# Angle tables through two matmuls, a gate with its key sums side by side, and constants built once, in an attention and long-convolution kernel

## The chip, the cores and the metric

One core of a Trainium2 chip runs the whole program. The core has five engines that work side by side, each through its own queue in order: PE (TensorE, matmuls), ACT (ScalarE, activations and copies), DVE (VectorE), POOL (GpSimd) and SP (SyncE), which here issues all transfers. The metric is the device time of one execution in microseconds (us).

## The reference

Inputs are q, k, v of shape (4, 8, 768, 64), w_proj (512, 1536), filter_fft (768, 512) and w_out (512, 512), all float32. The first half is block attention: each query may look at its own block of 64 keys and at the three earlier blocks whose mean key fits it best. The second half is a gated long convolution over the sequence.

```python
k_rep = k.reshape(B, H, n_blocks, 64, D).mean(axis=3)
gate = np.einsum('bhsd,bhnd->bhsn', q, k_rep)        # causal blocks only, others -1e9
top_idx = np.argsort(gate, axis=-1)[..., -3:]        # plus the query's own block
scores = where(mask & causal, scale * q @ k.T, -1e9)
x = softmax(scores) @ v                              # heads merged: (4, 768, 512)
x1, x2, x3 = split(x @ w_proj)
x2_conv = irfft(rfft(x2, axis=1) * rfft(filter_fft, axis=0))
out = (x1 * x2_conv * x3) @ w_out
```

## The kernel before

**Attention.** The work is cut into 16 groups: one batch and one pair of heads each, 768 queries and keys, 128 partitions. For each group the kernel transposes keys on PE (L368), sums each block of 64 keys on DVE (`ks`, L371), copies keys to a slot (`kt`, L381, on ACT), and does the like for queries (L432; high fp16 part `qh` L435 on ACT, low part `ql` L438 on DVE). Scores are matmuls (L568), the exponential is on ACT (L575), the causal triangle is cut by POOL (L580), and the values are multiplied on PE (L598) and normalised on DVE (L611).

**The gate.** Key sums are kept as a high and a low fp16 part in `km`; queries likewise in `qx`. For each group `e_gate` runs 20 matmuls (L490): five chunks of 128 queries, and for each the four products high-high, high-low, low-high and low-low, summed in one PSUM bank over 24 columns (12 blocks of two heads). `e_max` (L503 to L509) writes a large negative number over the blocks that aren't causal, in PSUM, and takes the eight largest of each row; `e_lt` (L516, L521) compares with the third largest and writes a mask of zeros and ones. The mask is transposed (L538) into 12 spare rows of the query slot (`qt`, L545). The key slot has the block pattern `eblk` in the same 12 rows, filled once with -30720 on the block's own columns (L206 to L209, copied by L226), so the score matmul adds the mask. Four slots of each kind exist. The first nine groups (`tm=9`) go this way; the last seven let DMA do the transposes (L470, L474).

**The tables.** `F` holds sines and cosines for a DFT of length 768, folded to 384 rows. Six pieces of 128 x 384 are made at the start, each in five steps: a matmul of row and column numbers gives the angle in units of 1/768 turn (e1, L253); multiply by 1/768 and add 2^23, which rounds to whole turns (e2, L258 on ACT or L261 on DVE); subtract 2^23 (e3, L267); angle minus 768 times the turns (e4, L272, DVE); sine (e5, L276, ACT). The steps e2 to e4 keep float32 in `prod` buffers. An exponential may start only when all of `F` is there, since sine and exponential need different tables on ACT.

**The convolution.** Each group's result goes through sums and differences (L636) and table matmuls (L648, L655) to a spectrum `XT`. When four groups, one batch, are there, the batch is projected (L757), multiplied with the filter's spectrum (L766, DVE), combined (`Y`, L776, POOL), transformed back (L820), combined again (`ce` L829, `sd` L835) and multiplied with the gating products (L793, L799, L802) into `yT` (L841, POOL or DVE), then projected out (L851), copied (L855) and stored (L858).

**The order.** A list scheduler in the kernel's Python, `plan`, orders all operations before the program is built. Each operation has a priority time `vt`, counted in groups, with a weight for its kind (`v_...`), a cost per engine, and for some kinds a choice of engine with a penalty for DVE (`d_...`). `ahead` bounds how far beyond the current score step operations may be taken. Buffers are pools with fixed counts (`POOLS`); PSUM has eight banks of which four serve all but the scores while attention runs. Until `warm_until` of planned time, `filler` puts matmuls of zeros (L952) where PE would have nothing to do.

Of the kernel before, what the change touches and what calls it, by code (L numbers as in the profile page):

```python
# [16 lines left out]
P = 128  # L17
# [15 lines left out]
MAGIC = float(2 ** 23)  # L33
# [11 lines left out]
for _pi, _segs in enumerate(PIECES):  # L45
# [6 lines left out]
    direct=2, tm=9, kin=16, p0=-2.58, p1=0.359, pvlag=-1.081, dlag=1.538, dlen=1.485, h0=4.836,  # L52
    hlen=3.401, f0=-0.546, f1=4.97, ld=-1.042, s2a=-0.355, s2b=0.464, x0=0.446, x1=1.137, c0=0.817,
    c1=1.054, o0=1.347, ahead=16.341, delta=0.011, queue=6.283, w0=1.608, wl=1.643, wlag=-7.304, warm_until=34.129,
    tr0=-26.33, trl=16.468, fill0=1.323, v_yT=1.15, v_sd=-2.381, d_k2=3.845, v_trig=4.775, v_ldq=-0.068, v_max=-6.527,
    v_g=2.311, v_Y=0.82, v_k2=0.404, v_rec=-2.613, v_small=3.535, v_gate=-0.028, v_km=1.623, d_x1=-0.346, d_shQ=0.734,
    v_xT=-2.135, v_prod=-3.254, v_ldv=-0.43, d_yT=0.279, v_ks=0.928, v_osb=-3.052, v_ldk=-0.329, v_kT=0.038, v_gT=3.039,
    d_md=0.144, d_trig=0.482, v_qT=0.017, v_mT=-0.085, v_lt=-3.096, v_fe=1.769, d_eo=0.005, v_md=0.045, v_phase=-0.03,
    v_shQ=2.489, v_ldf=0.595, d_Y=5.668, v_sel=-5.514, v_warm0=3.241, v_x1=-0.983, v_ldw=-0.146, v_tab=6.693, v_va=1.68,
    v_iota=-1.707, d_XT=-0.476, v_qh=0.233, v_h0=0.611, v_eblk=4.461, v_id32=1.695, v_st=2.959, v_nyq=-2.837, v_s2=0.062,  # L60
    v_st1=0.023, v_XT=0.064, v_t=-9.103, v_ql=1.449, v_hf=0.158, d_g=6.58, d_ce=8.444, d_osb=2.444, d_fill=0.427,
    v_w=-0.555, v_ce=-1.909, v_fill=-0.339, v_op=1.026, v_pv=-1.989, d_w=4.395, v_nrm=-0.253, v_ha=-5.02, v_id16=-0.109,
    v_eo=1.933, v_x13=-0.231, d_fe=-4.145, v_cv=-1.548, v_sc=0.113, v_T2=-0.349, v_T1=2.226, d_qh=2.343, v_pq=-4.162,
    d_pq=6.99, v_ex=0.251, a0=0.0, o1=1.0, pen_dve=0.205, late=2.0,
)

POOLS = dict(kn=2, qn=3, vn=2, k2=1, qx=4, ks=2, km=3, m8=2, nm=1,
# [16 lines left out]
class Op:  # L84
    __slots__ = ("i", "eng", "emit", "deps", "bufs", "alloc", "vt", "lock", "size", "tag",
                 "start", "done", "on", "pre", "nd", "succ", "ready")


class Graph:
# [3 lines left out]
    def add(self, tag, vt, eng, emit, rd=(), wr=(), res=(), lock=False, size=0):  # L93
        o = Op()
        vt += self.par.get("v_" + tag, 0.0)
        o.i, o.tag, o.vt, o.eng, o.emit, o.lock, o.size = len(self.ops), tag, vt, eng, emit, lock, size
        deps = set()
# [43 lines left out]
def build(par):  # L141
# [21 lines left out]

    def cviews(x):
        cv = x.rearrange("p (g n) -> p g n", g=2)
        return (cv[:, :, 0:256].rearrange("p g (k n) -> p g k n", k=2),
                cv[:, :, 256:HS].rearrange("p g (k n) -> p g k n", k=2))

    def e_warm0(E, nc, en):
        nc.vector.memset(E.warm, 0.0)  # L170
        nc.vector.memset(E.colv, 0.0)
        nc.vector.memset(E.rowv, 0.0)

    def e_phase(E, nc, en):
        ph = E.colv[32:33, :]
        nc.vector.memset(E.rowv[32:33, :], 1.0)
        nc.vector.memset(ph, 192.0)
        for x_ in cviews(ph):
            nc.vector.memset(x_[:, :, 1, :], 0.0)
        nc.vector.memset(ph[:, P:P + 1], 192.0)  # L180
        nc.vector.memset(E.magic, MAGIC)
        nc.vector.memset(E.nmagic, -MAGIC)
# [14 lines left out]
    add("warm0", T0 - 1, {"DVE": (0.6, 0.75)}, e_warm0, wr=[cb("warm"), cb("cols"), cb("phase")])  # L197
    add("tab", T0 - 1, {"ACT": (1.5, 1.6)}, e_tab, rd=[cb("warm")], wr=[cb("tab")])
    add("phase", T0, {"DVE": (1.62, 1.7)}, e_phase, wr=[cb("phase"), cb("magic")])
# [4 lines left out]
    def e_eblk(E, nc, en, h=0):  # L204
        x = E.eblk[64 * h:64 * h + 64, :]
# [6 lines left out]
    for h in range(2):  # L212
        add("eblk", T0 + 3 + h, {"POOL": pol(2.48)}, lambda E, nc, en, h=h: e_eblk(E, nc, en, h), wr=[(cb("eblk"), h)])

    slot_init = []
    for i in range(POOLS["kt"]):
# [5 lines left out]
        def e_fk(E, nc, en, i=i):  # L222
            eng = nc.vector if en == "DVE" else nc.gpsimd
            for h in range(2):
                r = slice(0, 64) if h == 0 else slice(64, 76)
                eng.tensor_copy(E.t["kt"][i][r, :, h, :], E.eblk[r, :].rearrange("p (c s) -> p c s", s=P))  # L226
# [4 lines left out]
                rd=[(cb("eblk"), 0), (cb("eblk"), 1)], wr=[(cb(("slot", i)), 1)], lock=True)])  # L231
# [13 lines left out]
    for t in range(HC):  # L245
        for hf in range(2):
            vt = par["tr0"] + par["trl"] * (0.33 * t + 0.16 * hf)
            pr, kk = psb(), Buf("prod")
            ka, kb = (kk, 0), (kk, 1)
# [5 lines left out]

            def e2(E, nc, en, pr=pr, kk=kk):
                if en == "ACT":
                    nc.scalar.activation(E.sb(kk)[:, 0:HS], E.bk(pr)[:, 0:HS], AF.Identity,  # L258
                                         bias=E.magic, scale=1.0 / S)
                else:  # L260
                    nc.vector.tensor_scalar(E.sb(kk)[:, 0:HS], in0=E.bk(pr)[:, 0:HS], scalar1=1.0 / S,  # L261
                                            scalar2=MAGIC, op0=ALU.mult, op1=ALU.add)

            def e3(E, nc, en, kk=kk):
                o, i_ = E.sb(kk)[:, HS:S], E.sb(kk)[:, 0:HS]
                if en == "ACT":
                    nc.scalar.activation(o, i_, AF.Identity, bias=E.nmagic, scale=1.0)  # L267
                else:
# [899 lines left out]
```

## Time and profile before

| | |
|---|---|
| median of 6 runs | 235.57 us (235.25 to 235.79) |
| profiled execution | 235.63 us, span 233.9 us |
| busy: PE, DVE, ACT, POOL | 227.3, 193.7, 174.6, 170.9 us |
| clock granted to PE | full in all of the span |
| DMA | 40.9 MB, 76.7% of 16 engines' span |
| PE fillers (L952) | 143, the last at 34.9 us |
| first exponential | 22.75 us |
| last matmul ends | 230.1 us |

The span runs from the first instruction to the last of one execution; the execution's own time is 1.7 us longer. Busy time counts an instruction from its start to its end, so overlapping ones make PE look fuller than its rate: 20 gate matmuls have a mean of 173 ns each, and together take 0.49 us.

### The profile page before, as it was taken

What the parts mean: (1) busy time and instruction counts of PE and PEld (TensorE: products, weight loads), DVE (VectorE), ACT (ScalarE), POOL (GpSimd) and SP (SyncE); (2) the same over time, 40 slices, a digit from 0 to 9 for tenths busy, and PEclk for the clock granted to TensorE, in tenths of its full rate; (3) what the DMA queues carried; (4) which work ended last, traced back from release to release, by engine and by line L of the source; (5) the groups of instructions that cost most, each with busy time, mean ns of one, the idle gap of its engine ahead of it and who ended that gap; (6) DMA issues with size and microseconds to landing.
All of it is one profiled execution on the core that took longest, in us unless ns stands there. A gap on an engine that the chain in (4) does not pass through costs nothing.

```text
span 233.9 us, 6574 instructions
## 1 busy us (share of the span) xinstructions
PE 227.3 (97%) x2370; PEld 157.7 (67%) x2370; DVE 193.7 (83%) x617; ACT 174.6 (75%) x288; POOL 170.9 (73%) x312
## 2 busy tenths in 40 slices
PE   8998999999999999999999999999999999999993
PEld 6897877777765777777656767776566677545551
DVE  6788988888799999899898889888996887596850
ACT  3989999999989889897967886967575656414243
POOL 8848967776549999998599999674699652169720
PEclk9999999999999999999999999999999999999999
DMA  6999996999999999999999999516185210512016
GB/s 179 320 233 226 236 243 189 228 195 211 247 221 223 266 211 235 243 188 176 264 217 275 166 261 169 123 36 158 49 169 160 67 34 3 168 53 86 0 45 224
DMA packets 120224, 40.92 MB, mean 175 GB/s; under 512 B 114304, under 2 KB 114304, under 8 KB 120192
## 3 DMA queue, kind: packets, MB, share of 16 engines
q1 hardware_dynamic: 120192, 40.51, 76.7%
q8 instruction: 18, 0.29, 0.5%
q14 instruction: 14, 0.11, 0.2%
HBM read 24.64 MB, written 6.29 MB: 132 GB/s over the span
## 4 chain that ended last, share of the span: by engine, by line
PE 78%; ACT 12%; DVE 4%; issue 2%; DMA 2%; POOL 0%; ACTq 0%; DVEq 0%; POOLq 0%; SPq 0%
PE ps L793 17%; PE ps L568 12%; PE ps L851 9%; PE ps L757 8%; PE ps L598 7%; PE ps L820 7%; ACT ex L575 6%; PE ps L952 5%; PE ps L648 4%; PE ps L368 3%; ACT kt L381 3%; PE ps L490 2%; PE ps L655 2%; DMA kn<-in_k_dram 2%; ACT qx L435 1%
## 5 line engine op out<-in xcount | busy, mean ns | idle before, releaser
L575 ACT ACTIVATE ex<-ps 128x1024 f16<-128x1024 f32 (+1 forms) x96 | 85.0, 924 | 10.4 <-PE ps L568 9.6
L580 POOL TENSOR_SCALAR_AFFINE_SELECT ex<-ex 128x256 f16<-128x256 f16 x96 | 42.9, 452 | 22.4 <-ACT ex L575 20.5
L568 PE MATMUL ps<-qt,kt 76*128 76x512 f16 (+7 forms) x256 | 49.8, 305 | 0.3
L776 POOL TENSOR_TENSOR Y<-t,t 128x512 f16<-128x512 f32 (+1 forms) x32 | 40.5, 1271 | 11.9 <-DVE t L766 10.9
L793 PE MATMUL ps<-xT,wp 128*128 128x384 f16 x256 | 48.9, 326 | 0.0
L381 ACT CAST kt<-ps 64x384 f16<-64x384 f32 x64 | 30.3, 474 | 9.9 <-PE ps L368 8.0
L793 PEld LDWEIGHTS <-wp 128*128 128x128 f16 x256 | 24.1, 98 | 14.2 <-issue 0.2
L568 PEld LDWEIGHTS <-kt 76*128 76x128 f16 (+1 forms) x256 | 23.4, 97 | 14.8 <-issue 1.0
L598 PEld LDWEIGHTS <-ex 128*128 128x128 f16 x672 | 25.2, 97 | 4.0 <-issue 0.9
L598 PE MATMUL ps<-va,ex 128*128 128x65 f16 x672 | 26.6, 193 | 0.3 <-DVE qt L545 0.2
L855 ACT COPY osb<-ps 128x512 f32<-128x512 f32 x24 | 14.1, 589 | 16.9 <-PE ps L851 16.8
L841 POOL TENSOR_TENSOR yT<-prod,sd 128x384 f16<-128x384 f32 x23 | 23.3, 1026 | 4.0 <-DVE prod L802 2.6
L851 PE MATMUL ps<-wo,yT 128*128 128x512 f16 x96 | 23.3, 379 | 0.0
L757 PE MATMUL ps<-wp,XT 128*128 128x512 f16 x96 | 23.2, 379 | 0.1
L802 DVE TENSOR_TENSOR prod<-ps,x 128x384 f32<-128x384 f32 x32 | 17.7, 553 | 5.1 <-PE ps L793 3.4
L952 PE MATMUL ps<-warm 128*128 128x256 f16 x143 | 20.5, 290 | 1.1 <-DVE warm L170 1.1
L371 DVE TENSOR_REDUCE ks<-ps 128x6 f32<-128x384 f32 x32 | 17.3, 550 | 2.2 <-ACT kt L381 1.7
L611 DVE TENSOR_TENSOR xn<-ps,rec 128x384 f16<-128x384 f32 x32 | 17.8, 556 | 0.9
L820 PE MATMUL ps<-G,Y 128*128 128x384 f16 x96 | 18.2, 326 | 0.0
L835 DVE TENSOR_TENSOR sd<-ce,ps 128x384 f32<-128x384 f32 x32 | 16.1, 550 | 2.0 <-ACT ce L829 1.3
L952 PEld LDWEIGHTS <-warm 128*128 128x128 f16 x143 | 14.6, 104 | 4.0 <-DVE warm L170 1.1
L766 DVE TENSOR_TENSOR t<-ps,HA 128x512 f32<-128x512 f32 x24 | 16.4, 685 | 0.9 <-PE ps L757 0.4
(109 smaller groups left out, 397.9 us busy)
## 6 DMA issues: line engine op xcount, KB each, us to landing
kn<-in_k_dram SPq DMA_DIRECT2D x32, 192.0 KB, 3.8
qn<-in_q_dram SPq DMA_DIRECT2D x32, 192.0 KB, 3.7
vn<-in_v_dram SPq DMA_DIRECT2D x16, 384.0 KB, 4.7
out_dram<-osb SPq DMA_DIRECT2D x24, 256.0 KB, 2.1
t<-in_moe_w_proj_dram SPq DMA_DIRECT2D x12, 256.0 KB, 3.9
t<-in_moe_filter_fft_dram SPq DMA_DIRECT2D x6, 256.0 KB, 4.6
qt<-qx SPq DMA_DIRECT2D x14, 96.0 KB, 3.6
t<-in_moe_w_out_dram SPq DMA_DIRECT2D x4, 256.0 KB, 4.1
```

Of the source, the lines that this page charges most:

```text
L381: (nc.scalar.copy if en == "ACT" else nc.vector.tensor_copy)(E.sb(Kt[g])[r, HC * hf:HC * (hf + 1), 1 - t, :], E.bk(kp)[r, 0:HS].rearrange( ...
L568: nc.tensor.matmul(o[:, col:col + w], lhsT=E.sb(Kt[g])[0:KR[t], kc, 1 - t, :], rhs=E.sb(Qt[g])[0:KR[t], q0 // P:(q0 + w) // P, 1 - t, :], ...
L575: nc.scalar.activation(E.sb(ex)[:, 0:w], E.sp(sp)[:, 0:w], AF.Exp, scale=ESC)
L580: nc.gpsimd.affine_select(out=dv, in_=dv, compare_op=ALU.is_ge, fill=0.0, base=0, pattern=[[0, 2], [1, P]], channel_multiplier=-1)
L598: nc.tensor.matmul(o[:, 65 * c:65 * c + 65], lhsT=E.sb(exs[pi])[:, col:col + P], rhs=E.sb(va[g])[:, t, kc, :], start=(kc == 0), stop=(kc = ...
L757: nc.tensor.matmul(E.bk(xa), lhsT=w, rhs=E.wp[:, j, Dm:2 * Dm], start=(j == 0), stop=(j == NP - 1))
L776: (nc.vector if en == "DVE" else nc.gpsimd).tensor_tensor(E.sb(Y)[ro, n_, :], E.sb(x)[ri, :], E.sb(y)[ri, :], op=op)
L793: nc.tensor.matmul(E.bk(xq)[:, 0:HS], lhsT=E.wp[:, d2, 2 * Dm * m + P * dc:2 * Dm * m + P * (dc + 1)], rhs=E.sb(xT[gs[d2]])[:, cs], start= ...
L820: nc.tensor.matmul(E.bk(cv)[:, 0:HS], lhsT=E.sb(Y)[:, 3 * p_ + n_, P * dc:P * (dc + 1)], rhs=E.G[:, 3 * p_ + n_, :], start=(n_ == 0), stop ...
L841: (nc.vector if en == "DVE" else nc.gpsimd).tensor_mul(E.sb(yT)[:, dc, cs], E.sb(prod)[:, cs], E.sb(sd)[:, cs])
L851: nc.tensor.matmul(E.bk(op_), lhsT=E.sb(yT)[:, d2, P * c:P * (c + 1)], rhs=E.wo[:, d2, :], start=(d2 == 0), stop=(d2 == NP - 1))
L952: nc.tensor.matmul(E.ps[:, 3584:3840], lhsT=E.warm[:, 0:P], rhs=E.warm[:, 0:256], start=True, stop=True)
```

## The change

*Tables.* A row of ones times 1536 turns is added to the angle by the first matmul (row 64 of `rowv` holds 1536 and rows 64 to 127 of `colv` hold 768). Divided by 768 and written as fp16, the value lies between 1024 and 2048, where fp16 has whole numbers only, so the write rounds to whole turns. A second matmul with -768 times the identity (`nid`) subtracts them in PSUM, and the sine reads PSUM. The rounded turns take an `x1` buffer in place of `prod`.

*Gate.* High and low key sums are the 48 columns of one operand, so a chunk takes two matmuls. A DVE reduction adds the two halves into a new SBUF tile `gs` (two buffers), on which the masking, MAX8 and comparison then work.

*Constants.* `eblk` has 64 rows instead of 128, is built once, and its rows are copied to the second half of the slots too. The fillers' operand is cleared ahead of all else.

*The plan.* Nearly every weight in `PAR` is another (a few are in the diff below). The cost model adds 0.115 us where ACT or DVE goes on to another partition quadrant, and some costs are changed.

```diff
-    hlen=3.401, f0=-0.546, f1=4.97, ... ahead=16.341, ... warm_until=34.129,
-    ... d_trig=0.482, ... d_yT=0.279, ... d_x1=-0.346, ... d_osb=2.444
+    hlen=3.36, f0=-1.155, f1=7.084, ... ahead=46.953, ... warm_until=32.306,
+    ... d_trig=6.615, ... d_yT=8.721, ... d_x1=3.233, ... d_osb=6.098
...
+    add("nid", T0 + 2.05, {"DVE": dve(64)}, lambda E, nc, en: nc.vector.tensor_scalar_mul(E.nid, E.id32, -float(S)),
+        rd=[cb("id32")], wr=[cb("nid")], lock=True)
...
-        nc.vector.memset(E.warm, 0.0)
-        nc.vector.memset(E.colv, 0.0)
+        nc.vector.memset(E.colv[0:64, :], 0.0)
+        nc.vector.memset(E.colv[64:P, :], float(S))
...
+        nc.vector.memset(E.rowv[64:65, :], TURNS)
...
-    for h in range(2):
-        add("eblk", T0 + 3 + h, {"POOL": pol(2.48)}, lambda E, nc, en, h=h: e_eblk(E, nc, en, h), wr=[(cb("eblk"), h)])
+    add("eblk", T0 + 3, {"POOL": pol(2.48)}, e_eblk, wr=[cb("eblk")])
...
-                r = slice(0, 64) if h == 0 else slice(64, 76)
-                eng.tensor_copy(E.t["kt"][i][r, :, h, :], E.eblk[r, :].rearrange("p (c s) -> p c s", s=P))
+                n_ = 64 if h == 0 else NB
+                eng.tensor_copy(E.t["kt"][i][64 * h:64 * h + n_, :, h, :],
+                                E.eblk[0:n_, :].rearrange("p (c s) -> p c s", s=P))
...
             def e2(E, nc, en, pr=pr, kk=kk):
                 if en == "ACT":
-                    nc.scalar.activation(E.sb(kk)[:, 0:HS], E.bk(pr)[:, 0:HS], AF.Identity,
-                                         bias=E.magic, scale=1.0 / S)
+                    nc.scalar.activation(E.sb(kk), E.bk(pr)[:, 0:HS], AF.Copy, bias=0.0, scale=1.0 / S)
...
+            def e3(E, nc, en, pr=pr, kk=kk):
+                nc.tensor.matmul(E.bk(pr)[:, 0:HS], lhsT=E.nid, rhs=E.sb(kk), start=False, stop=True,
+                                 skip_group_check=True)
+            def e5(E, nc, en, t=t, cs=cs, pr=pr):
+                nc.scalar.activation(E.F[:, t, cs], E.bk(pr)[:, 0:HS], AF.Sin, bias=0.0, scale=TWO_PI / S)
...
-                for n_, (lo, w) in enumerate(((0, 0), (0, 1), (1, 0), (1, 1))):
+                for lo in range(2):
                     col = P * (2 * (c - 1) + lo) if by_dma else S * lo + P * c
-                    nc.tensor.matmul(o[:, 32 * c:32 * c + 24], lhsT=E.sb(qs)[:, col:col + P],
-                                     rhs=E.sb(km)[:, w, 0:24], start=(n_ == 0), stop=(n_ == 3))
+                    nc.tensor.matmul(o[:, 64 * c:64 * c + 48], lhsT=E.sb(qs)[:, col:col + P],
+                                     rhs=E.sb(km)[:, 0:2, :], start=(lo == 0), stop=(lo == 1))
...
+            nc.vector.reduce_sum(x, o[:, :, 0:48].rearrange("p c (w n) -> p c n w", w=2), axis=AX.X)
+            nc.vector.memset(bass.AP(tensor=h, offset=off + 3, ap=[[row, 64], [26, 5], [12, 2]]), NEG)
...
-                    nc.vector.max(E.sb(m8)[:, c - 1, t, :], gv[:, c - 1, 12 * t:12 * t + n])
+                    nc.vector.max(E.sb(m8)[:, c - 1, t, :], x[:, c - 1, 12 * t:12 * t + n])
...
+        if e in quad and quad[e] != o.quad:
+            occ, vis = occ + 0.115, vis + 0.115
...
     with tc.manual_schedule():
+        nc.vector.memset(E.warm, 0.0)
         for o in order:
             o.emit(E, nc, o.on)
```

## The prediction

> **What bounds the kernel now.** I read four views, from coarse to fine. First the page's busy lines, then its 40 slices (one digit is 5.8 us, 9 means 90% or more):
>
> ```profile
> PE 227.3 (97%) x2370; PEld 157.7 (67%) x2370; DVE 193.7 (83%) x617; ACT 174.6 (75%) x288; POOL 170.9 (73%) x312
> PE   8998999999999999999999999999999999999993
> ACT  3989999999989889897967886967575656414243
> ```
>
> PE looks like the bound everywhere. But its 97% holds filler matmuls that compute nothing, and ACT is just as full in the first third. The groups by line give the filler and the rows that the change touches (columns: busy us, mean ns, idle time before):
>
> ```profile
> L952 PE MATMUL ps<-warm 128*128 128x256 f16 x143 | 20.5, 290 | 1.1 <-DVE warm L170 1.1
> L490 PE MATMUL ps<-km,qx 128*128 128x24 f16 x320 | 10.5, 173 | 0.0
> L509 DVE MAX8 m<-ps 128x8 f32<-128x8 f32 (+2 forms) x160 | 13.5, 161 | 0.6
> L267 ACT ACTIVATE prod<-prod,nmagic 128x384 f32<-128x384 f32 x6 | 3.3, 617 | 0.0
> L272 DVE SCALAR_TENSOR_TENSOR prod<-prod,ps 128x384 f32<-128x384 f32 x6 | 3.1, 553 | 0.6 <-ACT prod L267 0.6
> L276 ACT ACTIVATE F<-prod 128x384 f16<-128x384 f32 x6 | 2.9, 524 | 0.0
> ```
>
> All 143 fillers lie before 35 us; at 0.109 us each (the chain has 40 of them in 4.37 us) they fill 15.6 us of that time. The busy times by stretch (PE, PEld, DVE, ACT, POOL; then clock, DMA share, GB/s) show where each engine is the limit:
>
> ```profile
> 5.00:38.00 33.00, 32.22 (x356) 26.89 (x355) 27.79 (x96) 31.34 (x59) 25.02 (x49) 1.00 1.03 256
> 38.00:75.00 37.00, 36.16 (x487) 26.74 (x485) 32.40 (x126) 36.00 (x60) 25.22 (x55) 1.00 1.05 215
> 75.00:225.00 150.00, 149.95 (x1492) 99.01 (x1491) 128.82 (x374) 102.24 (x163) 116.48 (x199) 1.00 0.67 148
> ```
>
> Up to 38 us PE's work is largely filler and ACT is busy 31.3 of 33 us: ACT, with DVE behind it, sets the pace. From 38 to 75 us PE and ACT are both full. From 75 us to the last matmul at 230.1 us PE alone is. The chain of work that ended last says so for the end, all on PE:
>
> ```profile
> 222.34 2.60 PE ps L793 x16
> 224.94 5.19 PE ps L851 x24
> 230.14 0.03 ACTq L855
> ```
>
> So two things shorten this kernel: an earlier moment at which PE is full (38 us), and less PE work after it.
>
> **What the Trainium skill says.** (1) "TensorE: Matmul & The Clock Gate", section "Wait — 56ns, not 53.3ns?": matmuls start N/2.4 GHz + 2.5 ns apart, but never closer than about 25 ns. The trace agrees: the chain has "L490 x20" at 0.49 us, 24.5 ns each with 24 columns. With 48 columns the formula gives 22.5 ns, still under the floor, so a matmul twice as wide costs the same. (2) "ScalarE: Activation LUTs", section "What ACT_TABLE_LOAD costs": a per-partition bias operand adds about 93 ns. The trace: L258 (bias operand, float32 out) starts every 0.47 us, L435 (same size, no bias operand, 16-bit out) every 0.38 us. (3) "VectorE: DVE Perf Modes", table "The perf-mode tier table": tensor_reduce runs at one element per cycle at best. L371 agrees: 384 elements, 0.50 us from start to start, so about 0.10 us beside the 0.40 us of elements.
>
> **The change, part by part.**
>
> *Gate matmuls (L490).* Twenty per group become ten of 48 columns: 16 groups x 10 x 24.5 ns = 3.9 us of PE. By stretch there are 60, 80 and 180 matmuls before 38, in 38-75 and after 75 us, that is 3, 4 and 9 groups. The first three run among fillers: worth nothing. The nine save 9 x 0.245 = 2.2 us on the path. The four save 1.0 us of PE where ACT has only 1.0 of 37 us free; I count half, 0.5 us. Sum: 2.7 us.
>
> *Angle tables.* Before, each of six pieces was one matmul (L253), then multiply-and-round (L258 on ACT x4, L261 on DVE x2), subtract the constant (L267, ACT), multiply-add (L272, DVE), sine (L276, ACT). After: matmul, one fp16 copy, matmul with -768 times the identity, sine out of PSUM. ACT before, from start to start: 4 x 0.465 + 6 x 0.507 + 6 x 0.41 = 7.4 us. After, if all six copies go to ACT (the planner's penalty for DVE on these, d_trig, rises from 0.48 to 6.6): 12 x 0.38 = 4.6 us, from row L435. That is 2.8 us less on ACT; with two copies left on DVE, 3.6. DVE loses 6 x 0.50 + 2 x 0.50 = 4.0 us. PE gains 6 x 0.163 = 1.0 us between 6 and 15 us, where it runs 47 fillers between 9 and 15 us: nothing, as long as fillers are there. ACT was busy 16.6 of 17.4 us from its first key copy (5.39 us) to the first exponential (22.75 us), so most of the 2.8 us comes through. The change adds a wait: PE must wait for the copy before the second matmul, and behind it on PE stand the transposes of the first groups, which ACT and DVE wait for. Bounds: 0 if fillers cover each round trip, 6 x (0.38 + 0.16) = 3.2 us if none is. I take 0.6 us, one bare round trip for the last piece. Gain: 2.2 us, between 0 and 3.6.
>
> *Max and compare on DVE.* A reduction of 240 elements joins: 240/960 + 0.10 = 0.35 us per group. The ten MAX8 (0.085 us apart) and three memsets (0.145 us apart) now work in SBUF, and the bank is free after the reduction, some 1.5 us sooner. SBUF's access was not measured for these; bounds -0.4 and +0.1 us. Net +0.15 us, 2.4 us over 16 groups, against 4.0 us gone in the tables. DVE is 86% busy after 75 us and its results are not what PE waits for: nothing. In the start the group's chain gate, max, compare, mask copy grows by that 0.15 us; the freed DVE covers it.
>
> *Slot constants.* POOL builds one mask of 64 rows instead of two: 0.73 + 0.82 + 0.82 = 2.4 us less; the copies stay, one of them to other partitions. POOL then waits 3.0 us for a query copy (L415) anyway: nothing. The negated identity costs DVE about 0.5 us (like L161), extra constant memsets on one row about 0.4 us, magic 0.1 us less. They stand before the first angle matmul, whose inputs were ready at 5.23 us and which ran at 7.0. The filler's memset moved to the head saves at most the wait ahead of it: nothing.
>
> *The plan.* All weights of the list scheduler change, and its cost model gains 0.115 us for ACT and DVE when operands start in another partition quadrant. The trace shows that price: key copies on 64 partitions start 0.47 to 0.50 us apart, query copies of the same length on 128 partitions 0.38. It changes the plan, not the instructions; which order comes out cannot be read from the profile. Bounds: 1.5 us either way. I take 0. Loads keep their buffers and queue; SP issues the same 170 transfers in another order.
>
> **Sum.** 2.7 + 2.2 = 4.9 us. The profiled execution took 235.63 us (span 233.9, 1.7 around it), as good as the median of 235.57. 235.6 - 4.9 = **230.7 us**. With its bounds (start 0.9 to 3.6, order 1.2): 228.5 to 232.5.
>
> **Rivals.**
>
> *The start gives nothing.* DMA engines are full from 5 to 75 us (share 1.03 and 1.05), and the second pair's keys are transposed only at 16.3 us. If data or the DVE chain holds the first groups as long as ACT did, only the gates count: 235.6 - 2.7 = 232.9. For it: the DMA share. Against it: in 4-30 us ACT waited 3.5 us for key transposes, nearly all of it before 5.4 us, and nothing else waits for a load.
>
> *The end loses its cover (slower).* The last batch has a chain of its own: last spectrum copy (ends 204.2 us), then POOL's eight sums (L776, 206.6 to 216.9) and its products (L841, from 218.1, 0.97 us each), then the last output rows:
>
> ```profile
> 206.60 10.30 POOL L776 TENSOR_TENSOR Y<-t,t 128x512 f16<-128x512 f32 x8 [6.40 <-DVE t L766]
> 218.11 5.79 POOL L841 TENSOR_TENSOR yT<-prod,sd 128x384 f16<-128x384 f32 x6 [1.21 <-DVE sd L835]
> ```
>
> DVE made two of the eight products there; d_yT goes from 0.28 to 8.7, so POOL will make all: until 218.1 + 8 x 0.97 = 225.8. Then come half of the output matmuls (2.6) and the last copy and store (230.1 to 233.9, 3.8): 232.2, so the span can't end before the last spectrum copy + 28.0 us. It fits today (232.2 against 233.9). The look-ahead of the plan goes from 16 to 47 groups; if that pulls the 64 gating matmuls of the last batch (10.4 us) ahead of its last spectra, these come at 204.2 - 4.9 + 10.4 = 209.7, the span ends at 237.7 and the run at 239.4 us. It decides from a last spectrum copy after 205.9 us on.
>
> *The change does less than it says.* If the wider gates ran at 48 ns each, or the table's round trips stalled PE for all they can, and the order cost 1.5 us, it stays at 235.6.
>
> **How the numbers follow.** Likeliest case 0.60 (230.7), start lost 0.21 (232.9), no change 0.04, slower 0.15. About 0.2% (0.5 us) is what a measurement of this kernel can tell from no change. Faster 0.81, same 0.04, slower 0.15. The range takes the first two cases with 1.5 us of order below the lower one's middle, and reaches up past no change: 227.8 to 236.0.
>
> **What would show it.** Right: L490 with 160 matmuls and 0.245 us per group in the chain; the first exponential near 20.5 us instead of 22.75; PE without fillers and full from about 36 us; ACT's table rows near 4.6 us; last matmul near 225.3. Wrong: a first exponential still at 22 us or later, PE idle between 75 us and the end, or POOL's last product ending where PE waits for it.

## The result, and the profile after

The changed kernel takes **233.67 us** (median of 15 runs, 232.82 to 235.91); the kernel before, beside it, 235.57. The ratio is 0.9919 (95% interval 0.9905 to 0.9933): 1.9 us faster, where 4.9 were forecast. The time lies within the forecast range, but 3.0 of the 4.9 us are missing. The profiled execution took 234.07 us, span 232.4.

The page of the kernel after, in the rows shown of before (busy us and instructions; the 40 slices, one digit 5.8 us; the DMA queue: packets, MB, share of 16 engines):

```profile
PE 222.7 (96%) x2189; PEld 150.5 (65%) x2189; DVE 183.8 (79%) x615; ACT 175.8 (76%) x295; POOL 169.4 (73%) x309
PE   7999999999897999999999999999999999999993
ACT  3888999999977798899957887999476775405343
q1 hardware_dynamic: 120192, 40.51, 90.5%
```

PE falls to 8 and 7 in two slices, 58 to 64 and 70 to 76 us, where it had 9s before. DVE has 9.9 us less, ACT 1.2 us more. The same packets and bytes keep the DMA engines busy for 90.5% instead of 76.7% of the span; what this goes with is shown below. Groups of the kernel after (busy us, mean ns, idle before):

```profile
L945 PE MATMUL ps<-warm 128*128 128x256 f16 x116 | 18.1, 291 | 1.1 <-DVE warm L1133 1.1
L483 PE MATMUL ps<-km,qx 128*128 128x48 f16 x160 | 6.6, 183 | 0.0
L266 PE MATMUL ps<-x,nid 128*128 128x384 f16 x6 | 2.0, 326 | 0.0
```

The gate has its 160 matmuls, the tables their six more. In time order on ACT, the last sine of the tables and the first exponential:

```profile
11.29 0.56 ACT L270 ACTIVATE F<-ps 128x384 f16<-128x384 f32 x1
...
21.67 1.28 ACT L565 ACT_TABLE_LOAD   x1
22.97 1.02 ACT L565 ACTIVATE ex<-ps 128x1024 f16<-128x1024 f32 x1
```

The tables are ready at 11.85 us instead of about 15.6, but the first exponential starts at 22.97, not sooner than before (22.75). In the time won ACT and PE do the filter's spectra (L707 and L697), which the old order had later.

So is the start's gain real? I counted PE's work in both traces: every matmul but the fillers, once each, with the start-to-start time of its shape. At 40 us 187.5 us of work remain before and 181.7 after; at 60 us 169.3 and 165.3; at 80 us 150.2 and 148.6; at the end the last matmul of after is 1.5 us ahead. So the changed kernel was 5.8 us ahead at 40 us, 4.0 at 60 and 1.6 at 80.

Part of that lead is gate matmuls that are still to come and take less time. The changed kernel with the narrow gate matmuls put back (*oldgate_in_new*, described below) has 184.7, 167.7 and 150.6 us of work left at the same three times. Measured by it, the start's own lead over the kernel before is 2.8 us at 40 us and 1.6 at 60, and at 80 us it has become a lag of 0.4. The start's gain was there, more than the 2.2 us forecast, and was lost between 40 and 80 us. The stretches show where (busy us of PE, of its weight loads PEld, of DVE, ACT and POOL; then clock, DMA share, GB/s). Before:

```profile
40.00:60.00 20.00, 19.57 (x270) 14.62 (x268) 17.04 (x79) 19.81 (x34) 14.30 (x31) 1.00 1.07 208
60.00:80.00 20.00, 19.75 (x222) 13.74 (x219) 17.94 (x50) 19.18 (x32) 13.91 (x27) 1.00 1.09 239
```

After:

```profile
40.00:60.00 20.00, 18.69 (x246) 13.81 (x245) 16.59 (x72) 19.74 (x33) 16.40 (x37) 1.00 1.31 222
60.00:80.00 20.00, 17.65 (x201) 11.92 (x199) 17.26 (x64) 16.95 (x29) 15.08 (x29) 1.00 1.20 212
```

From 40 to 60 us ACT is full in both (19.8 and 19.7 of 20): PE's lead beyond ACT's is no use. This is read from the busy times and was not tested. From 60 to 80 us neither is full after: PE 17.65, ACT 16.95. PE in that stretch, with what ended its longer gaps:

```profile
63.90 0.87 PE L360 MATMUL ps<-id,kn 128*128 128x128 f32 x6 [0.74 <-DMA kn<-in_k_dram]
...
72.83 0.85 PE L360 MATMUL ps<-id,kn 128*128 128x128 f32 x6 [0.61 <-DMA kn<-in_k_dram]
```

It waits for keys, 1.3 us in all. Before, the keys of groups 6, 7 and 8 landed 5.5, 3.5 and 4.7 us ahead of their transposes; after, 0.3, 0.0 and 0.1. The kernel came earlier to a stretch that its loads do not reach earlier.

The loads themselves also take longer: 4.3 us in the median from the issue of a key load to its landing, instead of 3.8. This goes with the tables, not with the new order. All ten kernels traced with the old tables keep the DMA engines busy for 69.5% to 77.6% of the span; all ten with the new tables, whatever their order and gate, for 79.3% to 90.5%. Two kernels that differ in nothing but the tables, both with the new gate in the old order, from 80 to 120 us, first with the old tables (*gate_in_old*, below), then with the new (*both_in_old*):

```profile
80.00:120.00 40.00, 39.56 (x422) 27.24 (x419) 37.63 (x134) 33.75 (x57) 34.61 (x74) 1.00 1.04 216
```

```profile
80.00:120.00 40.00, 39.55 (x408) 27.19 (x407) 37.90 (x134) 33.51 (x57) 34.84 (x70) 1.00 1.34 218
```

The GB/s are the same and the share is not, so a share near 1, which the prediction read as full, was no ceiling. Of the 111104 packets of 256 bytes in each of the two kernels, 94% take 18 ns or less with the old tables and 60% with the new; packets of 2048 bytes take about as long in both (99 and 97 ns). The tables alone in the old order (*table_in_old*, below) show what comes of it: PE is 0.4 us behind the kernel before and not ahead of it, and yet the keys of group 8 land under 1 us ahead of their transposes instead of 5. What in the tables' code does this is not shown. Their last sine is over by 15 us, and the difference stays.

### The profile page after: what moved, and what is told of

It is laid out like the page before. It is cut to its first block, busy times and chain, and to the rows that moved or that the text cites. A ratio compares the mean times of both kernels' runs of the same rounds, so it can differ in the third digit from the quotient of the medians.

```text
span 232.4 us, 6222 instructions
## 1 busy us (share of the span) xinstructions
PE 222.7 (96%) x2189; PEld 150.5 (65%) x2189; DVE 183.8 (79%) x615; ACT 175.8 (76%) x295; POOL 169.4 (73%) x309
## 2 busy tenths in 40 slices
DMA packets 120223, 40.91 MB, mean 176 GB/s; under 512 B 114304, under 2 KB 114304, under 8 KB 120192
## 3 DMA queue, kind: packets, MB, share of 16 engines
q1 hardware_dynamic: 120192, 40.51, 90.5%
## 4 chain that ended last, share of the span: by engine, by line
PE 62%; DVE 7%; ACT 4%; DMA 2%; issue 2%; POOL 1%; SPq 0%; DVEq 0%; ACTq 0%; POOLq 0%
PE ps L783 15%; PE ps L558 9%; PE ps L841 9%; PE ps L747 7%; PE ps L810 6%; PE ps L588 6%; PE ps L638 4%; ACT ex L565 2%; DMA kn<-in_k_dram 2%; PE ps L645 2%; PE ps L360 2%; DVE t L756 1%; ACT kt L373 1%; DVE ks L363 1%; PE ps L483 1%
## 5 line engine op out<-in xcount | busy, mean ns | idle before, releaser
L565 ACT ACTIVATE ex<-ps 128x1024 f16<-128x1024 f32 (+1 forms) x96 | 86.3, 924 | 16.5 <-PE ps L558 15.9
L570 POOL TENSOR_SCALAR_AFFINE_SELECT ex<-ex 128x256 f16<-128x256 f16 x96 | 40.2, 426 | 23.4 <-ACT ex L565 21.6
L558 PE MATMUL ps<-qt,kt 76*128 76x512 f16 (+7 forms) x256 | 50.6, 305 | 0.8 <-ACT ex L565 0.5
L783 PE MATMUL ps<-xT,wp 128*128 128x384 f16 x256 | 49.8, 325 | 0.0
L831 POOL TENSOR_TENSOR yT<-prod,sd 128x384 f16<-128x384 f32 x32 | 32.2, 1017 | 3.6 <-DVE sd L825 2.3
L789 ACT CAST x<-ps 128x384 f16<-128x384 f32 x32 | 15.3, 478 | 14.1 <-PE ps L783 12.5
L747 PE MATMUL ps<-wp,XT 128*128 128x512 f16 x96 | 22.5, 379 | 0.1
L651 DVE CAST XT<-ps 128x256 f16<-128x256 f32 (+1 forms) x30 | 16.1, 545 | 5.6 <-PE ps L645 3.6
L845 ACT COPY osb<-ps 128x512 f32<-128x512 f32 x24 | 14.1, 590 | 8.3 <-PE ps L841 7.9
L945 PE MATMUL ps<-warm 128*128 128x256 f16 x116 | 18.1, 291 | 1.1 <-DVE warm L1133 1.1
L810 PE MATMUL ps<-G,Y 128*128 128x384 f16 x96 | 19.0, 326 | 0.0
```

The source lines that it names most:

```text
L558: nc.tensor.matmul(o[:, col:col + w], lhsT=E.sb(Kt[g])[0:KR[t], kc, 1 - t, :], rhs=E.sb(Qt[g])[0:KR[t], q0 // P:(q0 + w) // P, 1 - t, :], ...
L565: nc.scalar.activation(E.sb(ex)[:, 0:w], E.sp(sp)[:, 0:w], AF.Exp, scale=ESC)
L570: nc.gpsimd.affine_select(out=dv, in_=dv, compare_op=ALU.is_ge, fill=0.0, base=0, pattern=[[0, 2], [1, P]], channel_multiplier=-1)
L747: nc.tensor.matmul(E.bk(xa), lhsT=w, rhs=E.wp[:, j, Dm:2 * Dm], start=(j == 0), stop=(j == NP - 1))
L783: nc.tensor.matmul(E.bk(xq)[:, 0:HS], lhsT=E.wp[:, d2, 2 * Dm * m + P * dc:2 * Dm * m + P * (dc + 1)], rhs=E.sb(xT[gs[d2]])[:, cs], start= ...
L810: nc.tensor.matmul(E.bk(cv)[:, 0:HS], lhsT=E.sb(Y)[:, 3 * p_ + n_, P * dc:P * (dc + 1)], rhs=E.G[:, 3 * p_ + n_, :], start=(n_ == 0), stop ...
```

## The experiments

"Old order" below is the kernel before with its plan untouched and only the named code replaced; matmuls can then be compared one by one with the kernel before, and "behind" means later than the same matmul there.

**One part at a time.** *gate_in_old* has the new gate's matmuls, reduction, MAX8 and compare in the old order:

```diff
-                for n_, (lo, w) in enumerate(((0, 0), (0, 1), (1, 0), (1, 1))):
...
+                for lo in range(2):
...
+                    nc.tensor.matmul(o[:, 64 * c:64 * c + 48], lhsT=E.sb(qs)[:, col:col + P],
+                                     rhs=E.sb(km)[:, 0:2, :], start=(lo == 0), stop=(lo == 1))
...
+            nc.vector.reduce_sum(x, o[:, :, 0:48].rearrange("p c (w n) -> p c n w", w=2), axis=AX.X)
```

> The kernel before, with its order of operations kept exactly; only the gate is new (two matmuls of 48 columns per chunk, a DVE reduction into SBUF, masking, MAX8 and comparison there). Theory A (each edit is worth what was counted, and the changed kernel's new order of work and loads gives part of it back): 2.7 us less than before, 232.9. Theory B (transfers were at their limit up to 80 us, so whatever lets the start run ahead is eaten by late loads, in any order): the nine late groups' 2.2 us and perhaps less, 233.4 to 234.5. Theory C (the reduction and the longer chain on DVE take back what PE saves): 235 or more.

*table_in_old* has the new tables in the old order, with nothing left of the fourth step (`e4`):

```diff
+                nc.tensor.matmul(E.bk(pr)[:, 0:HS], lhsT=E.nid, rhs=E.tq[kk.slot], start=False, stop=True,
...
-                nc.vector.scalar_tensor_tensor(out=E.sb(kk)[:, HS:S], in0=E.sb(kk)[:, HS:S], scalar=-float(S),
-                                               in1=E.bk(pr)[:, 0:HS], op0=ALU.mult, op1=ALU.add)
```

> The kernel before, order kept; only the angle tables are new (fp16 copy in place of the multiply-and-round, second matmul at the place where the subtraction stood, nothing where the multiply-add stood, sine out of PSUM). The first exponential should come some 2 us sooner than at 22.75 us. Theory A: 2.2 us less, 233.4. Theory B: the start is sooner, but a load comes late between 40 and 80 us and PE stands idle there: 0 to 1 us less. Theory C': the round trips through PE hold ACT up, and the first exponential is not sooner: no change.

*both_in_old* has both. *oldgate_in_new* is the changed kernel with 20 narrow gate matmuls again (its reduction becomes a copy of the same place):

> The kernel before, order kept, with the new gate and the new tables together: all of the change that PE, ACT and DVE compute, without the new plan and the new constants. Theory A: 4.9 us less than before, 230.7, so 3 us faster than the changed kernel. Theory B: about as fast as the changed kernel, 233.0 to 234.2, with PE idle between 40 and 80 us behind key loads. Theory C: 235 or more.

> The changed kernel, order kept, with 20 gate matmuls of 24 columns per group put back; DVE copies the 24 columns into its SBUF tile in place of the reduction, so all else stays. It tells what the narrower gate is worth in the new order. Theory A: PE work grows by 3.9 us, of which the nine late groups' 2.2 us show in full and the middle four in part: 2.2 to 2.7 us over the changed kernel, 235.9 to 236.4. Theory B: between 40 and 80 us PE stands idle anyway, so only the nine late groups: 2.2 us, 235.9. Theory C: little or no difference from the changed kernel, since DVE's chain is the limit.

Measured: gate_in_old 238.28 us (ratio 1.0106, 1.0088 to 1.0125), table_in_old 236.79 (1.0053, 1.0032 to 1.0075), both_in_old 237.01 (1.0057, 1.0042 to 1.0072), oldgate_in_new 236.38 (1.0020, 1.0002 to 1.0038). In the old order each part makes the kernel slower. In the new order the wide gate matmuls are worth 236.38 - 233.67 = 2.7 us by the medians, 2.4 by the ratios. In the two traces, matmul by matmul, the kernel with narrow ones is level with the changed kernel at 76 us. From there on it falls back by about 0.25 us at each of the nine groups that are left, 2.3 us in all, and by 0.5 us more at two places near 98 and 109 us that are no gates. So the late groups are worth what was counted, and the middle groups show nothing. The tables, the constants and the new plan together cost 0.8 us (0.5 by the ratio, with an interval from 0.0 to 0.9) instead of gaining 2.2.

**Why the gate loses in the old order.** Of gate_in_old's lag 1.5 us have arisen by 34 us; up to 88 us it stays at 1.5. Later each group's 0.245 is won, and given back at PE's next wait for DVE. After 88 us the lag grows by 1.1 us more, 1.0 of it at one product at 144 us. There the compare ahead of the product takes 0.63 us instead of 0.28, and the DVE operation behind the compare (L465, which has both inputs in SBUF too) 1.39 instead of 0.82, both while POOL works in SBUF. The first part has a visible cause. DVE, POOL and PE of gate_in_old around 26 us, one fence each:

```profile
26.50 0.87 DVE L513 TENSOR_TENSOR nm<-gs,m 128x120 f16<-128x120 f32 x1
```

```profile
26.41 1.68 POOL L226 COPY kt<-eblk 64x768 f16<-64x768 f16 x2
```

```profile
27.73 0.45 PE L535 MATMUL ps<-id,nm 128*128 128x128 f16 x5 [0.88 <-DVE nm L518]
```

The compare takes 0.87 us where it took 0.28, while POOL copies slot constants; the mask transposes wait for it. In the kernel before they stood only 0.27 and 0.13 us behind the end of the compare's chain in the first two groups, so nothing is left to absorb it. The compare used to have one input in PSUM; now both, `gs` and `m`, are in SBUF. The groups of before and of gate_in_old:

```profile
L516 DVE TENSOR_TENSOR nm<-ps,m 128x120 f16<-128x120 f32 x9 | 2.4, 269 | 0.1
L516 DVE TENSOR_TENSOR qx<-ps,m 128x120 f16<-128x120 f32 x7 | 1.9, 277 | 0.0
```

```profile
L513 DVE TENSOR_TENSOR qx<-gs,m 128x120 f16<-128x120 f32 x7 | 4.5, 645 | 0.0
L513 DVE TENSOR_TENSOR nm<-gs,m 128x120 f16<-128x120 f32 x9 | 4.3, 473 | 0.1
```

The Trainium skill says this in "SBUF — State Buffer", section "Who interferes with whom": a DVE instruction with two SBUF inputs contends with a GpSimd instruction that reads SBUF, and issue order decides who blocks. The traces agree. In all runs together 65 compares with two SBUF inputs take more than 0.5 us, and every one of them ends 0.12 to 0.14 us after the end of a POOL instruction that had started before it. The 144 compares with one input in PSUM take at most 0.28 us. both_in_old shows the other outcome at the same place. There the compare starts 0.1 us ahead of the copy:

```profile
25.81 0.28 DVE L510 TENSOR_TENSOR nm<-gs,m 128x120 f16<-128x120 f32 x1
```

```profile
25.91 2.09 POOL L230 COPY kt<-eblk 64x768 f16<-64x768 f16 x2
```

and the kernel is 0.2 us behind at 34 us instead of 1.5, though it does the same gate; in time it ends 1.3 us below gate_in_old.

Does the held compare explain all of it? *gate_psum_in_old* puts the sums back into the bank, so that the compare has one SBUF input again:

```diff
-            x = E.gs[m8.slot]
+            x = E.bk(gn)[:, 384:504].rearrange("p (c n) -> p c n", n=24)
```

> The kernel before, order kept, with the 48-column gate, but the reduction writes back into spare columns of the same PSUM bank, and masking, MAX8 and comparison work there as before. So the comparison again has one input in PSUM and one in SBUF. Theory P (in the old order the new gate lost 2.7 us because the comparison, now with two SBUF inputs, is held for up to 0.6 us while POOL works in SBUF): the comparison takes 0.28 us each time, and the time falls from 238.3 to near or under the kernel before, 233.5 to 236. Theory Q (the loss comes from the reduction and DVE's fixed order alone): still 237.5 or more, since the reduction stays and the PSUM memsets are slower.

240.79 us (1.0220, 1.0198 to 1.0242). The compare is never held (0.24 to 0.28 us), and the time is still worse. Here the reduction comes on top of masking and MAX8 at their old price, about 0.45 us per group, so the chain is longer in every group. A longer chain costs as well as a held compare.

Hence the dose test. *before_more_dve* and *after_more_dve* do five of the ten MAX8 twice, and nothing else:

```diff
-                    nc.vector.max(E.sb(m8)[:, c - 1, t, :], gv[:, c - 1, 12 * t:12 * t + n])
+                    for _ in range(2 - t):
+                        nc.vector.max(E.sb(m8)[:, c - 1, t, :], gv[:, c - 1, 12 * t:12 * t + n])
```

> The kernel before, with five of the ten MAX8 of every group done twice (same values): about 5 x 0.085 = 0.42 us more of DVE per group, 6.8 us over 16 groups, in the same place of the chain where the new gate's reduction stands. Theory (in the old order DVE is late for PE, so what the gate adds on DVE is paid): slower by 1.5 us or more, 237.1 to 240. Rival (the prediction's 'nothing': PE does not wait for DVE's results): within 0.5 us of 235.6.

> The changed kernel with the same five MAX8 done twice: 5 x 0.079 = 0.40 us more of DVE per group. Theory (the new order moved some 10 us of other work off DVE, so it has room): slower than the changed kernel by less than half of what the kernel before loses, 233.7 to 234.6. Rival (DVE is as late in the new order): the same loss as in the kernel before. Second rival (DVE never matters): within 0.5 us of 233.7.

Measured: 249.68 us (1.0589, 1.0548 to 1.0630) and 242.07 (1.0251, 1.0211 to 1.0291). The dose was larger than planned: a row of MAX8 took 1.89 instead of 0.84 us and 1.82 instead of 0.79, so five cost 1.05 and 1.03 us per group, 16.8 and 16.5 us in all. The groups of the two:

```profile
L510 DVE MAX8 m<-ps 128x8 f32<-128x8 f32 (+2 forms) x240 | 27.5, 164 | 3.3
```

```profile
L501 DVE MAX8 m<-gs 128x8 f32<-128x8 f32 (+2 forms) x240 | 26.3, 160 | 3.0
```

Against their own kernels they lose 14.1 of 16.8 us (84%) and 8.4 of 16.5 us (51%). By the numbers expected, the loss of the new order is too large; by the ratio, it is still more than half. So the prediction's "nothing" for DVE's part of the gate is wrong in both orders, and the new order has more room, not enough. The dose is long and stands in the chain of each group; the slope for 0.13 us may be smaller.

Is it DVE's load as a whole? The new plan has 17 copies and nine products fewer on DVE. *gate_moved* moves 24 of them in the old order, *before_moved* is its control:

```diff
+    for o in order:
+        if o.tag == "x1":
+            o.on = "ACT"
+        if o.tag == "yT" and o.start < 200.0:
+            o.on = "POOL"
```

> The new gate alone in the old order, with the same 24 operations moved off DVE. Theory (in the old order the new gate loses because DVE is late for PE): the loss of 2.7 us goes and the gain of the narrower work on PE appears, 233.5 to 235.0. Rival (the loss comes from something that goes with the gate itself, such as its compare being held by POOL or the longer chain of each group): 237.5 or more.

> Control: the kernel before with 17 copies of x1 moved from DVE to ACT and 7 products yT of the first three batches from DVE to POOL, in the same places of the order, as the new plan has them: about 17 x 0.50 + 7 x 0.53 = 12.2 us less on DVE. PE has no gaps after 75 us there, so both theories expect nothing: within 0.5 us of 235.6.

239.20 us (1.0141, 1.0123 to 1.0160) and 236.69 (1.0042, 1.0028 to 1.0057). The control became slower by 1.1 us, and the gate costs 2.5 us against it, as before (2.7). **As an account of the whole loss, the theory of DVE's total load fell**: 11.9 us less DVE work brought back 0.2 us, no more than the noise. The moved work all lies after 72 us, so the 1.5 us that arise by 34 us were out of its reach.

Then it is the first groups' chain? *gate_masks_later* and its control move the mask transposes and mask copies of groups 0 and 1 behind more of PE's instructions:

```diff
+    for g, n in ((0, 5), (1, 10)):
+        moved = [masks[g]] + copies[2 * g:2 * g + 2]
+        behind = [o for o in order[order.index(moved[0]) + 1:] if o.on == "PE"][n - 1]
...
+        order[at:at] = moved
```

> The new gate alone in the old order (238.3), with the mask transposes and mask copies of the first two groups moved behind five and ten more instructions of PE (mostly fillers, 0.7 and 1.4 us). Theory (the first two groups' transposes stand 0.27 and 0.13 us behind the end of the compare in the old order, so what the new gate adds to the chain of gate, maxima and compare is paid at once by PE, and ACT, full from 34 to 75 us, carries the 1.5 us on): PE is at most 0.5 us behind the kernel before at 34 us instead of 1.5, time 236.9 to 237.6. Rival (the delay comes from elsewhere, such as the extra DVE work as a whole): 1.2 us or more behind at 34 us, time 237.9 or more.

> Control: the kernel before with the same moves. There the transposes do not wait for the compare, so both theories expect nothing: 235.6 within 0.4.

238.15 us (1.0104, 1.0086 to 1.0122) and 236.62 (1.0043, 1.0028 to 1.0057). By its time this is the rival's number. The control was no bystander: a key transpose then waited for the moved copies. Against it the gate now costs 1.5 us instead of 2.7, and 0.7 instead of 1.5 at 34 us. About half of the early loss thus belongs to those two transposes; the other half came out at the next work that waits for DVE (ACT's key copies behind DVE's key sums). What is shown: in the old order the gate pays at the results of DVE that stand closest ahead of PE in the first 34 us, held compares included. Of the 1.1 us after 88 us, nearly all comes at 144 us, with the two held operations named above.

**Why the tables bring no earlier exponential.** In table_in_old ACT is busy 27.8 of the 33 us from 5 to 38 us instead of 31.3: 3.5 us less, as counted. But it waits for PE. ACT of table_in_old (last brackets: idle before, and what ended it):

```profile
12.90 1.09 ACT L274 ACTIVATE F<-ps 128x384 f16<-128x384 f32 x2 [1.09 <-PE ps L267]
...
16.67 0.48 ACT L683 COPY G<-ps 128x384 f16<-128x384 f16 x1 [1.91 <-PE ps L679]
```

Its first exponential starts at 23.59, 0.8 us later than before. The fillers are instructions in an order made before the program runs: PE executes all 40 that stand between the last angle matmul and L679, whoever waits. *table_less_fill* leaves the last 20 of them out, *before_less_fill* is its control:

```diff
+    at = order.index(next(o for o in order if o.tag == "gT" and o.on == "PE"))
+    for o in [o for o in order[:at] if o.tag == "wm"][-20:]:
+        order.remove(o)
```

> The new tables alone in the old order, without the same 20 fillers. Theory (the number of fillers is written into the order, so in the old order PE's six added matmuls come on top of them and ACT's saving is lost waiting for PE): the filter transposes start some 1.5 to 2.2 us sooner than 16.3, the first exponential at 22.6 or sooner instead of 23.6, time 235.7 to 236.2 instead of 236.8. Rival (loads or the DVE chain hold the first groups): first exponential within 0.3 us of 23.6, time 236.8 within 0.3.

> Control: the kernel before without the last 20 of the 40 filler matmuls that stand ahead of the first filter transpose (20 x 0.109 = 2.2 us of PE). There PE's fillers end just as the last sine ends, so without them PE waits for it: both theories expect no change, 235.6 within 0.3, first exponential at 22.7.

235.08 us (0.9990, 0.9972 to 1.0009) and 236.12 (1.0012, 0.9990 to 1.0033). By the medians the tables win 1.7 us without the 20 fillers, 1.5 by the ratios, and the control wins nothing. The medians flatter this. The 16 executions of table_in_old lie in two clusters, eight from 235.99 to 236.39 us and eight from 237.19 to 238.64; of the 22 of table_less_fill 16 lie from 234.77 to 235.60 and six from 236.09 to 237.07. From the lower cluster of the one to that of the other it is 1.2 us. The traces say the same for PE at 34 us: 0.4 us behind the kernel before with the fillers, 0.8 ahead without them. ACT of table_less_fill:

```profile
20.63 1.28 ACT L572 ACT_TABLE_LOAD   x1
21.92 1.02 ACT L572 ACTIVATE ex<-ps 128x1024 f16<-128x1024 f32 x1
```

The exponential comes 1.7 us sooner than with the fillers and 0.8 sooner than before. The profiled execution is one of the slower six (236.85 us). In it the 0.8 us lasts to 60 us; then PE waits 0.78 us for DVE at 61 us and 0.62 for a key load at 66, and the lead is gone: the same stretch as in the changed kernel. Eight executions took 234.77 to 234.81 us, which is the kernel before's time less the 0.8 us, so these may have kept the lead to the end; none of them was traced.

*both_less_fill* takes the fillers out beside both parts, *both_moved_less_fill* also moves the 24 operations:

> Both parts in the old order (237.0) without the 20 filler matmuls. If the filler's cost is the same as beside the tables alone (1.7 us): 235.3; if DVE, later with the new gate, takes its place: 236.5 or more.

> Both parts in the old order, with the 24 operations moved off DVE and without the 20 filler matmuls: the old order with the three hindrances that the runs point to taken away. If they add up, 237.0 - 1.7 - 3.5 = about 232, below the changed kernel's 233.7; if the loads at 60 to 80 us limit it as they limit the changed kernel, 233 to 234.5; if neither matters here, 236 or more.

237.47 us (1.0072, 1.0056 to 1.0089) and 237.89 (1.0092, 1.0073 to 1.0111). The remedies do not add up. In both_less_fill PE is 2.2 us sooner at 14 us, then the start shifts under POOL's copies: the compare of group 1 takes 0.86 us, the mask transposes wait 0.88, and at 34 us it is 0.5 us later than both_in_old.

**Whether loads took the rest.** *after_less_v* is the changed kernel without the value loads of groups 3 to 9, so those values are stale; *before_less_v* is its control:

```diff
+            if 3 <= g <= 9:
+                return
```

> The changed kernel, order kept, without the value loads of groups 3 to 9 (seven transfers of 384 KB, in the stretch from 25 to 85 us; those groups use values that an earlier group left, so this part of the work is left out). Theory L (the start's gain is lost between 60 and 80 us because key loads land just as PE wants them, and the transfers are at their limit): keys of groups 6 to 8 land some microseconds before their transposes again, PE's holes from 40 to 80 us shrink, 1.5 to 3 us less than the changed kernel, 230.7 to 232.2. Theory M (PE waits there for ACT or DVE and the loads only look late): no more than 0.5 us less.

> Control: the kernel before without the same seven value loads (that part of the work is left out). Its keys land 3.5 to 9.5 us before their transposes, so theory L expects no gain: 235.2 to 235.7. If less load traffic alone makes any order faster, it gains as much as the changed kernel does.

232.84 us (0.9875, 0.9854 to 0.9896) and 235.64 (1.0004, 0.9992 to 1.0016): 0.8 us for the changed kernel (1.0 by the ratios), nothing for the kernel before. Keys 6 to 8 have 2.9 to 5.1 us of slack again. The stretch from 60 to 80 us of after_less_v, to be laid beside the one above:

```profile
60.00:80.00 20.00, 19.51 (x216) 13.35 (x214) 19.26 (x68) 18.13 (x31) 16.60 (x31) 1.00 0.82 178
```

PE is busy 19.51 us instead of 17.65. At 77 us it is 2.1 us ahead of the changed kernel; 1.0 us goes again between 85 and 95 us, where PE waits for POOL's causal masks and sums (L572 and L768). Behind the loads stands POOL.

*after_keys_first* issues the key loads of groups 6 to 8 as early as their buffers allow:

```diff
+        at = order.index(turned[2 * g - 3]) + 1
+        order[at:at] = keys[2 * g:2 * g + 2]
```

> The changed kernel; only six transfers move in SP's queue: the key loads of groups 6, 7 and 8 are issued as soon as their buffer is free (after the transposes of groups 4, 5 and 6), ahead of projection-weight loads and transposes that stood before them. Theory L in the form 'the order of the loads': the keys land some microseconds sooner and 1.5 to 2.5 us are won, 231.2 to 232.2. Theory L in the form 'the amount of transfers': what is moved back is late instead (weights, queries), and it stays within 0.7 us of the changed kernel. Theory M: no change.

235.02 us (0.9971, 0.9955 to 0.9987), 1.3 us slower than the changed kernel. The keys have 8 to 13 us of slack, and between 66 and 77 us PE wins back 1.3 us. But other transfers are late instead: POOL waits 4.4 us for projection weights between 40 and 68 us, instead of 2.3, PE waits 2.0 us for POOL's causal masks, and 1.5 us are lost between 46 and 66 us. After 85 us another 0.9 us go. It is the transfers up to there as a whole, not the order of the keys alone. No version of mine that computes everything beats the changed kernel.

## Why the prediction was right or wrong

- **Gate matmuls, 2.7 us: right in size, in part by luck.** 2.7 us were measured in the new order (2.4 by the ratios). The nine late groups gave 2.3 where 2.2 were counted. The four middle ones, counted at half, show nothing, and the other 0.5 us comes from waits that were not in the sum. In the old order the same edit, with its work on DVE, loses 2.7 us, which the step had no term for.
- **Max and compare on DVE, "nothing": wrong.** The size was good where nothing holds the compare: 1.69 us from the start of the reduction to the end of the compare, where it was 1.56 from the first masking, so +0.13 against +0.15. Two things failed. "Its results are not what PE waits for" was read from a stretch in which PE has no gaps; that PE does not wait does not say by how much it does not, and the margin was 0.13 us at one place. And the bounds (-0.4 to +0.1 us) left out that POOL can hold an operation with both inputs in SBUF: +0.6 to +0.7 us. The section of the Trainium skill named above says that such an operation contends with POOL, and the prediction did not draw on it.
- **Tables, 2.2 us: the term for ACT was right (3.5 us less with two copies left on DVE), its passage to the path was wrong.** The prediction let PE's six matmuls cost "nothing, as long as fillers are there". Fillers do not give way; their number is part of the order. In the old order the saving is lost there; in the new one it becomes earlier filter work, and a lead that is there at 40 us (2.8 us, with all else that the new order does to the start).
- **Earlier start means earlier end: wrong, and this is the step that cost the forecast.** The start's 2.2 us were carried to the end in full. The lead of 2.8 us at 40 us was gone at 80. "Nothing else waits for a load" held for the old pace and the old transfers. With PE 4.0 us ahead at 60 us the keys arrive just in time, PE waits 1.3 us for them, and 2.4 of the 4.0 us go by 80 us. And the transfers were put at nothing, because they "keep their buffers and queue"; with the new tables the same packets take the engines 90.5% of the span instead of 76.7%. Seven loads fewer give 0.8 us back. How the rest divides between the earlier pace, the longer transfers, ACT before 60 us and POOL after 85 us stays open. This is the first rival's mechanism, some 40 us later than it was placed. That rival's time, 232.9, lies nearer to the 233.67 than the forecast's.
- **The plan, taken as 0:** with old-width gates the new kernel stands at +0.8 us (+0.5 by the ratio), including the tables. Since the tables alone in the old order give between +1.2 and -0.5, the plan by itself is not separated.
- **The end's cover, the slower rival:** its mechanism did not set in. The last spectrum copy ends at 202.7 us, before 205.9; PE waits 0.3 us, once, for POOL's products.
- **Constants, nothing:** not tried by themselves.
- **The range of the sum, 228.5 to 232.5, was narrower than its own terms:** 0 to 3.6 us for the start and 1.5 us either way for the order give 227.8 to 234.4, which holds the measured time.

## What to carry to other kernels

In a hand-made order an operation's cost depends on the margin between its result and the next consumer: read that margin (here 0.13 to 3.8 us), not only whether the consumer waits today. A filler is work in a fixed order, not slack; count it out when work is added beside it. An earlier start is worth what the next limit downstream lets through, so check how far ahead of use each load lands before a gain is counted. An edit that touches no transfer can still make transfers longer: compare their times before and after, too. And when the executions of one kernel fall into clusters, ask from which of them the trace is.

## What the runs showed of the hardware

- A compare of 128x120 float32 with both inputs in SBUF takes 0.28 us alone and up to 1.03 us when it starts while POOL is at an instruction in SBUF; it then ends 0.12 to 0.14 us after that instruction (65 of 65). With one input in PSUM it never took longer than 0.28 (144 of 144). When it started 0.1 us ahead of the POOL copy, it took 0.28.
- MAX8 writing the same eight values again costs 0.21 us for each repetition, against 0.085 for a new place. I took 0.085 for the dose, and it was 2.5 times as large.
- Small memsets start 0.015 us apart in SBUF, where those in PSUM started 0.145 apart; ten MAX8 take 0.79 us from SBUF and 0.84 from PSUM.
- The same 120192 packets and 40.51 MB occupied the DMA engines for 69.5% to 77.6% of the span in nine kernels with the old tables and for 85.1% to 90.5% in nine with the new ones (70.1% and 79.3% with seven loads fewer). 256-byte packets took 18 ns or less in 94% or 95% of cases with the old tables, in 58% to 67% with the new. Why, no run here shows.
